# First batch's normalisation in two operations, its dilated values used where they land, one tail load a batch, and a new table of biases

## The chip, the cores and the metric

The kernel runs on one core of one Trainium2 chip. The metric is the device time of one execution in microseconds, median of the runs. Five engines work side by side, each through its own queue of instructions in order: TensorE (PE; its weight loads are shown apart as PEld), VectorE (DVE), ScalarE (ACT), GpSimd (POOL) and SyncE (SP). Loads are issued by POOL or SP and carried out by 16 DMA engines.

## The reference, cut to what matters

Attention over 8 batches, 8 heads, 576 positions and 64 columns a head, followed by a gated two-layer network over the 4608 tokens. Heads 0 to 3 see the 32 last positions ("plain"), heads 4 to 7 every fourth of the last 128 ("dilated").

```python
mask_plain = (rel >= 0) & (rel < 32)
mask_dil = (rel >= 0) & (rel < 128) & (rel % 4 == 0)
...
scores = np.where(masks, q @ k.T / 8, -1e9)
attn = np.exp(scores - max); attn = attn / (attn.sum() + 1e-9)
x = attn @ v                               # to (4608, 512)
h = x @ w_in                               # 512 x 2048
out = (h / (1 + np.exp(-beta * h))) @ w_out    # 2048 x 512
```

## The kernel before, in words

All products are in bf16. The network works on nine tiles of 512 tokens. For each, `slot_h` (L892) makes 16 blocks of 128 of the 2048 hidden columns: four products with w_in (L901) into a bank of PSUM, a tanh on ACT (L910), a gate on DVE (L915). `block` (L924, `block_cols` L930) makes four blocks of 128 tokens of the output: 16 products with w_out (L936) in four parts, an evacuation (L951 or L953) and a store from SP (L956). For the first four blocks of the first tile, `slot_h` splits its products in three: rows 2 and 3 of xT (the dilated heads) first, then rows 0 and 1 for the first 288 columns, then for the rest, so that it can start before all of batch 0's attention is done.

`attention` (L551) computes one batch into xT, which is the network's transposed input. The steps bear names: K and Q are transposes of keys and queries on PE (L483 dilated, L493 plain) and their copies out of PSUM (L257); S are scores (L697 dilated, L761 plain, T at L666 for the tail, the last 16 positions of each of the four dilated streams) with an exponential on ACT (L633) and, from batch 1 on, a mask on DVE or POOL (L637). Batch 0 gets its mask as a product with an identity instead (L687, L747, L750). V are the products of the weights with the values (L802 dilated, L818 plain), U those of the tail (L787). The values have a column of ones behind their 64 columns, so the 65th column of the product is the sum of the weights. `normed` (L644) then makes, on DVE and as one operation, a reciprocal of that column (L652) and a product with it (L653). In the first two batches X and Y transpose the result on PE (L855, L870, L840) and copy it into xT (L257); later ones go by DMA.

The values come in three ways. `direct_vp` (L430) loads the plain ones and copies a halo of 32 rows. `direct_vd` (L446) loads the dilated ones into vd16, 64 columns wide without ones, and `spread` (L619) copies them into vd, whose rows are 80 wide and have the ones; for the tail it issues two small loads into vt, one for each of two residues (L449). All these loads are issued by POOL (L408). Batches 0 to 2 load keys and queries straight into st; in batch 0 the first keys come by SP. The w_in matrix comes in three loads (L967), w_out in two halves (L972).

The order of all this is not written out. Each operation is registered in a list with the engines that may do it and their costs, its dependences and a due time (vt). `Plan.run` (L73) plays the list through on a model: among the operations that could start on an engine within about 50 ns of the first, the one with the smallest due time is taken, and where an operation may run on two engines, that one is open which ends at most 100 ns behind the other. `NUDGE` (L48) adds a bias in ns to the start at which an operation is compared; its key is the operation's place in the order of registration. A load counts eight earlier loads of its queue: it waits for the eighth before it to have landed. Where PE would be idle early on, the planner puts in fillers, products of zeros (L1057, L1059). The due times of batch 0's loads are those in L963 to L976: w_in -7.3, -7.29, -7.28, w_out -7.235 and -7.19. Those of batch 1's come from `loads` (L999): first keys -7.25, first queries -7.24, plain keys -7.23, plain queries -7.22, dilated values -7.2. Number 199 of the list is batch 1's load of the plain queries, with a bias of -900; number 32 is the small identity ident_f, with -2500.

Of the kernel before, what the change touches and what calls it, by code (L numbers as in the profile page):

```python
# [40 lines left out]
class Plan:  # L41
# [6 lines left out]
    NUDGE = {6: 2500, 32: -2500, 44: 150, 45: -400, 58: -150, 72: 60, 76: -400, 88: -400, 96: 60,  # L48
        98: 150, 104: -2500, 105: 900, 107: 900, 161: 150, 167: 900, 172: 60, 173: 400, 199: -900,
        208: 150, 214: -400, 216: 2500, 221: 900, 223: 150, 234: -400, 238: -150, 239: 150,  # L50
        241: 150, 248: -60, 250: -2500, 257: -400, 259: -400, 264: 60, 275: 900, 277: 400,
        278: -2500, 279: 400, 292: -150, 311: 900, 318: -400, 323: 150, 326: -900, 329: 400,
        333: -400, 337: 60, 342: -900, 347: -400, 363: 2500, 364: -900, 365: -150, 367: -2500,
        372: 400, 379: 60, 380: -400, 383: -150, 390: 400, 392: -2500, 394: -400, 408: -150,
        415: -900, 425: -150, 494: -900, 500: -150, 519: 60, 526: 900, 528: -60, 529: 900,
        535: 900, 538: 2500, 553: 900, 589: -60, 597: -2500, 633: 2500, 661: -900, 663: 400,
        669: 2500, 671: 2500, 680: 400, 681: -400, 684: 150, 685: -150, 807: 400, 916: -60,
        943: 150, 948: 150, 1083: 2500}
# [140 lines left out]
def kernel(  # L199
# [215 lines left out]
    def direct_qk(b, z, h0, deps, vt):  # L415
        rows, n, dst = ((2 * GD, RD, std) if h0 else (P, RP, stp))
        src = bass.AP(tensor=(k, q)[z].tensor, offset=(k, q)[z][b, h0].offset,
                      ap=[[n * D, rows], [2 * S * D, 2], [1, n * D]])
        return load("POOL", (dst[z], src), deps, vt, 576, .41 if b or not (z and h0) else .29, lat=1100 if b else 1450)
# [26 lines left out]
    def direct_vd(b, deps, vt, tdeps=()):  # L446
        src = v[b, 4:8].rearrange("h (t T) d -> t h (T d)", T=C)[0:P]
        out = [load("POOL", (vd16_of[b].rearrange("p h T d -> p h (T d)"), src), deps, vt, 512, .39, lat=1450 if b < DIRECT else 4000, late=0 if b <= DIRECT else 4000)]
        for c in range(2):  # L449
            src = bass.AP(tensor=v.tensor, offset=v[b, 4].offset + ((P - WIN) * C + c) * D,  # L450
                          ap=[[2 * D, 2 * KTL], [S * D, 4], [1, D]])
# [51 lines left out]
    def war(*keys):  # L503
        return [o for key in keys for o in last.get(key, ())]
# [588 lines left out]
```

## Time and profile before

| | |
|---|---|
| median of 3 runs | 299.92 us (299.8 to 299.94) |
| the profiled execution | 299.95 us |
| its span | 298.3 us, granted clock 0.999 |
| TensorE busy | 293.0 us |
| VectorE, ScalarE, GpSimd busy | 186.1, 169.8, 90.4 us |
| products with w_in (L901), with w_out (L936) | 134.8, 136.6 us |
| DMA | 42.00 MB, mean 141 GB/s |

Times of rows are in microseconds from the start of the span; "x" is a count of instructions. A row of the timeline gives start, length, engine, line, operation and what it writes and reads; in brackets the idle time before it and what ended that. The chain that ended last is the sequence of work followed back from the end, each step to what released it. Lengths of products are records that overlap, so a group of four with 512 columns is listed as 1.04 us in the timeline and takes 0.86 us in the chain.

The loads of POOL land one behind the other; by their completion times in the trace (us): first queries 7.44, plain keys 8.95, plain queries 10.34, dilated values 11.74, plain values 12.67 and 13.64, w_in's first part 16.50, batch 1's plain queries 17.99, w_in's second and third part 20.50 and 25.43, batch 1's dilated keys 26.84, batch 0's two tail loads 27.18 and 27.56, batch 1's dilated queries 28.94, w_out's first half 34.77, batch 1's plain keys 36.01 and dilated values 37.33, w_out's second half 42.44.

### The profile page before, as it was taken

The page shows a single profiled execution, that of the slowest core. Times are in us where ns is not written, and L with a number is a line of the kernel's source. Part 1 is how long each engine was busy: PE and PEld are TensorE (multiplying, and loading weights), DVE is VectorE, ACT ScalarE, POOL GpSimd, SP SyncE. Part 2 cuts the span into 40 slices and gives each one's busy share as a digit, 9 for nine tenths or more (in the row PEclk, how much of TensorE's full clock was granted, in tenths as well). Part 3 has the DMA queues.
Part 4 walks back from the last instruction along what each step waited for, and adds up shares of the span by engine and source line. Part 5 has one row for each costly group of instructions (what it writes and reads, how often), then busy time and mean ns, then how long its engine had stood idle before and what let it go on. Part 6 is the DMA issues. An engine that isn't in the chain of part 4 may idle for free.

```text
span 298.3 us, 6224 instructions
## 1 busy us (share of the span) xinstructions
PE 293.0 (98%) x2424; PEld 149.8 (50%) x2424; DVE 186.1 (62%) x422; ACT 169.8 (57%) x308; POOL 90.4 (30%) x126
## 2 busy tenths in 40 slices
PE   8999999999999999999999999999999999999995
PEld 6765456545554445444544454445444444444454
DVE  4879668888767658774589358936891075433300
ACT  3768876867456738642487348634862376445311
POOL 8987354654283026600551065000100000000000
PEclk9999999999999999999999999999999999999999
DMA  7999999999979995999999989995115200010122
GB/s 150 187 208 202 206 196 210 154 163 184 185 124 226 151 199 124 171 136 240 184 188 155 200 174 196 162 186 147 38 31 124 73 0 36 35 37 37 63 76 73
DMA packets 111249, 42.00 MB, mean 141 GB/s; under 512 B 87620, under 2 KB 104596, under 8 KB 111220
## 3 DMA queue, kind: packets, MB, share of 16 engines
q0 software_dynamic: 60336, 18.58, 59.6%
q1 hardware_dynamic: 50740, 22.95, 36.4%
q8 instruction: 19, 0.31, 0.4%
q10 hardware_dynamic: 144, 0.07, 0.1%
q14 instruction: 10, 0.08, 0.1%
HBM read 37.76 MB, written 18.87 MB: 190 GB/s over the span
## 4 chain that ended last, share of the span: by engine, by line
PE 86%; DMA 8%; POOL 2%; DVE 1%; issue 1%; ACT 0%; POOLq 0%
PE bank L936 42%; PE bank L901 36%; DMA w_out_bf<-in_moe_w_out_dram 6%; DMA w_in_bf<-in_moe_w_in_dram 2%; PE bank L818 2%; PE bank L697 1%; PE bank L802 1%; PE bank L725 1%; POOL vp L408 1%; PE bank L787 1%; PE bank L666 0%; PE bank L761 0%; POOL st L408 0%; DVE g L915 0%; PE bank L493 0%
## 5 line engine op out<-in xcount | busy, mean ns | idle before, releaser
L936 PE MATMUL bank<-w_out_bf,g 128*128 128x512 bf16 (+2 forms) x608 | 136.6, 368 | 0.4 <-DMA w_out_bf<-in_moe_w_out_dram 0.4
L901 PE MATMUL bank<-xT,w_in_bf 128*128 128x512 bf16 (+2 forms) x584 | 134.8, 376 | 0.1
L915 DVE SCALAR_TENSOR_TENSOR g<-tnh,bank 128x512 bf16<-128x512 bf16 x144 | 96.5, 683 | 51.5 <-ACT tnh L910 50.3
L910 ACT ACTIVATE tnh<-bank,beta_half 128x512 bf16<-128x512 f32 x144 | 98.4, 690 | 53.2 <-PE bank L901 47.4
L901 PEld LDWEIGHTS <-w_in_bf 128*128 128x128 bf16 x584 | 55.1, 98 | 60.6 <-issue 0.2
L936 PEld LDWEIGHTS <-g 128*128 128x128 bf16 x608 | 55.2, 98 | 57.8 <-DMA w_out_bf<-in_moe_w_out_dram 0.5
L951 ACT ACTIVATE osb<-bank 128x512 f32<-128x512 f32 (+1 forms) x30 | 17.6, 592 | 34.1 <-PE bank L936 29.5
L633 ACT ACTIVATE ptd<-bank 128x512 bf16<-128x512 f32 x32 | 17.0, 600 | 21.4 <-PE bank L697 21.4
L633 ACT ACTIVATE pt<-bank 128x384 bf16<-128x384 f32 (+1 forms) x54 | 21.1, 463 | 6.5 <-PE bank L725 4.1
L637 DVE TENSOR_TENSOR pt<-pt,mask_n 128x384 bf16<-128x384 bf16 (+1 forms) x39 | 14.5, 378 | 12.1 <-ACT pt L633 11.6
L653 DVE TENSOR_TENSOR xsp<-bank,rcp 96x384 bf16<-96x384 f32 x32 | 17.7, 554 | 1.1
L637 DVE TENSOR_TENSOR ptd<-ptd,mask_d 128x512 bf16<-128x512 bf16 x25 | 10.9, 448 | 11.3 <-ACT ptd L633 10.4
L953 DVE TENSOR_SCALAR osb<-bank 128x512 f32<-128x512 f32 (+2 forms) x8 | 4.9, 607 | 20.5 <-PE bank L936 20.5
L652 DVE RECIPROCAL rcp<-bank 128x4 f32<-128x4 f32 (+2 forms) x72 | 12.8, 177 | 3.5 <-PE bank L818 1.4
L408 POOL DMA_DIRECT2D vt<-in_v_dram x16 | 13.7, 864 | 4.0 <-DMA w_out_bf<-in_moe_w_out_dram 2.9
L637 POOL TENSOR_TENSOR pt<-pt,mask_n 128x288 bf16<-128x288 bf16 (+1 forms) x7 | 5.3, 764 | 31.2 <-ACT pt L633 31.2
L653 DVE TENSOR_TENSOR xdm<-bank,rcp 128x256 bf16<-128x256 f32 x32 | 13.6, 424 | 1.1
L408 POOL DMA_DIRECT2D s<-in_k_dram x10 | 12.9, 1286 | 0.6 <-issue 0.6
L1015 POOL COPY pace<-xT 1x2 bf16<-1x2 bf16 x4 | 0.7, 176 | 39.2 <-DMA xT<-x 39.2
L408 POOL DMA_DIRECT2D s<-in_q_dram x10 | 12.2, 1220 | 0.1
L818 PEld LDWEIGHTS <-pt 128*128 128x128 bf16 x192 | 8.9, 97 | 4.4
L408 POOL DMA_DIRECT2D vp<-in_v_dram x9 | 10.2, 1129 | 1.0 <-DVE g L915 0.8
(113 smaller groups left out, 186.8 us busy)
## 6 DMA issues: line engine op xcount, KB each, us to landing
out_dram<-osb SPq DMA_DIRECT2D x35, 256.0 KB, 3.8
s<-in_q_dram POOLq DMA_DIRECT2D x10, 288.0 KB, 10.2
s<-in_k_dram POOLq DMA_DIRECT2D x10, 288.0 KB, 9.0
w_out_bf<-in_moe_w_out_dram POOLq DMA_DIRECT2D x2, 1024.0 KB, 17.4
vp<-in_v_dram POOLq DMA_DIRECT2D x7, 288.0 KB, 13.5
st<-in_q_dram POOLq DMA_DIRECT2D x6, 288.0 KB, 10.0
x<-xsp SPq DMA_DIRECT2D x12, 144.0 KB
st<-in_k_dram POOLq DMA_DIRECT2D x5, 288.0 KB, 13.2
```

Source lines behind the costliest of these rows:

```text
L408: {"POOL": nc.gpsimd, "SP": nc.sync}[queue].dma_start(out=out, in_=in_)
L633: nc.scalar.activation(out=w(), in_=sc(), func=ACT.Exp, scale=SCALE)
L637: E[e].tensor_tensor(out=w(), in0=w(), in1=m(), op=ALU.mult)
L652: nc.vector.reciprocal(out=r, in_=p[..., D])
L653: nc.vector.tensor_tensor(out=dst, in0=p[..., 0:D], in1=r.unsqueeze(len(p.shape) - 1).to_broadcast(list(p.shape[:-1]) + [D]), op=ALU.mult)
L818: nc.tensor.matmul(pv[:, a, h2, :], lhsT=lhs, rhs=vp[kv][:, (2 * x + h2) * NI + 3 * j + a, 0:D + 1], start=True, stop=True)
L901: nc.tensor.matmul(bank(g)[:, a:z], lhsT=w_in_bf[:, kt, fb * P:(fb + 1) * P], rhs=xT[:, kt, xo + a:xo + z], start=(i == 0 and kt == kts[0] ...
L910: nc.scalar.activation(out=th[:, 0:n], in_=bank(g)[:, 0:n], func=ACT.Tanh, scale=beta_half[:, fb:fb + 1])
L915: nc.vector.scalar_tensor_tensor(out=g_t[t % 2][:, fb, c0:c0 + n], in0=th[:, 0:n], scalar=1.0, in1=bank(g)[:, 0:n], op0=ALU.add, op1=ALU.mult)
L936: nc.tensor.matmul(bank(g)[:, lo:hi], lhsT=g_t[t % 2][:, fb, tb * P:(tb + 1) * P], rhs=w_out_bf[:, fb, lo:hi], start=(fb == 0), stop=(fb = ...
L951: nc.scalar.mul(out=ob[:, lo:hi], in_=bank(g)[:, lo:hi], mul=0.5)
L953: nc.vector.tensor_single_scalar(out=ob[:, lo:hi], in_=bank(g)[:, lo:hi], scalar=0.5, op=ALU.mult)
```

## The change

In batch 0 alone, the spread is left out: the dilated products read vd16 where the load put it, 64 columns wide, and a second product of one column, with the ones of vd, makes the sum. In batch 0 alone, `normed` registers the reciprocal and the product as two operations, and the product may also run on ACT, one instruction for each block of 64 columns. In all batches the two tail loads become one. Two rates by which the planner reckons loads of later batches are changed, and the table of biases is replaced as a whole, since the places in the list shift: by -1 behind the merged load of batch 0, by -2 behind its spread, and by up to +7 behind its nine split norms. In the new table neither ident_f nor batch 1's plain queries (now number 206) has an entry; batch 1's tail load (now 208) has 150.

```diff
-    NUDGE = {6: 2500, 32: -2500, 44: 150, 45: -400, 58: -150, 72: 60, 76: -400, 88: -400, 96: 60,
-        98: 150, 104: -2500, 105: 900, 107: 900, 161: 150, 167: 900, 172: 60, 173: 400, 199: -900,
...
+    NUDGE = {54: -900, 57: 60, 58: -150, 63: -60, 67: -150, 68: -150, 69: -60, 75: 900, 77: 400, 91: 60,
+        93: -2500, 95: -900, 97: -60, 121: 60, 125: 60, 139: -2500, 140: 150, 143: 60, 146: 60,
+        152: 150, 156: -400, 167: -60, 175: 900, 188: -60, 208: 150, 214: 400, 219: 400, 221: 150,
...
-        return load("POOL", (dst[z], src), deps, vt, 576, .41 if b or not (z and h0) else .29, lat=1100 if b else 1450)
+        return load("POOL", (dst[z], src), deps, vt, 576, .36 if b > 1 else .41 if b or not (z and h0) else .29, lat=1100 if b else 1450)
...
-        for c in range(2):
-            src = bass.AP(tensor=v.tensor, offset=v[b, 4].offset + ((P - WIN) * C + c) * D,
-                          ap=[[2 * D, 2 * KTL], [S * D, 4], [1, D]])
-            out.append(load("POOL", (vt_[b % 2][:, c, :, 0:D], src), list(tdeps), vt + (1.255 if b == 0 else .02 if b < DIRECT else 0) + .001 + .001 * c, 96, .3, lat=1100 if b < DIRECT else 4000, late=0 if b <= DIRECT else 4000))
+        src = bass.AP(tensor=v.tensor, offset=v[b, 4].offset + (P - WIN) * C * D,
+                      ap=[[2 * D, 2 * KTL], [D, 2], [S * D, 4], [1, D]])
+        out.append(load("POOL", (vt_[b % 2][:, :, :, 0:D], src), list(tdeps),
+                        vt + (1.255 if b == 0 else .02 if b < DIRECT else 0) + .001, 192, .3,
+                        lat=1100 if b < DIRECT else 4000, late=0 if b <= DIRECT else 4000))
...
-        o = plan.op([("POOL", 1100), ("DVE", 620), ("ACT", 1030)], spread,
-                    [ld["vd"][0], (fill3, fill4)[kv]] + war(("vd", kv)), vt, sbuf=True)
-        used("vd16" if b < DIRECT else ("st", kv), o)
-        wrote(("vd", kv))
-        vdeps["D"] = [o]
+        if b:
+            o = plan.op([("POOL", 1100), ("DVE", 620), ("ACT", 1030)], spread,
+                        [ld["vd"][0], (fill3, fill4)[kv]] + war(("vd", kv)), vt, sbuf=True)
+            used("vd16" if b < DIRECT else ("st", kv), o)
+            wrote(("vd", kv))
+            vdeps["D"] = [o]
+        else:
+            vdeps["D"] = [ld["vd"][0], fill3]
...
+            if b == 0:
+
+                def inverse(e):
+                    p = pv()
+                    nc.vector.reciprocal(out=flat if len(p.shape) == 3 else flat.rearrange("p (m h) -> p m h", h=2), in_=p[..., D])
+                inv = plan.op([("DVE", 150)], inverse, [vop], vt - .003, group=g)
+
+                def scaled(e):
+                    p, to = pv(), dst
+                    r = flat if len(p.shape) == 3 else flat.rearrange("p (m h) -> p m h", h=2)
+                    if e == "DVE":
+                        nc.vector.tensor_tensor(out=to, in0=p[..., 0:D],
+                                                in1=r.unsqueeze(len(p.shape) - 1).to_broadcast(list(p.shape[:-1]) + [D]),
+                                                op=ALU.mult)
+                        return
+                    for i in range(blocks):
+                        at = (i,) if len(p.shape) == 3 else divmod(i, 2)
+                        at = (slice(None),) + tuple(at)
+                        nc.scalar.activation(out=to[at], in_=p[at][:, 0:D], func=ACT.Copy, scale=flat[:, i:i + 1])
+                vdone[key] = plan.op([("DVE", 160 + 1.042 * blocks * D), ("ACT", 235 * blocks)], scaled,
+                                     [inv] + war(war_key), vt - .003, group=g)
+                return
...
-                            nc.tensor.matmul(pv[:, r, a], lhsT=ptd[:, x - 2, j, 2 * r + a],
-                                             rhs=vd[kv][:, 2 * (x - 2) + a, 2 * r + j, 0:D + 1],
+                            lhs, at = ptd[:, x - 2, j, 2 * r + a], (slice(0, P), 2 * (x - 2) + a, 2 * r + j)
+                            if b:
+                                nc.tensor.matmul(pv[:, r, a], lhsT=lhs, rhs=vd[kv][at][:, 0:D + 1], start=True, stop=True)
+                                continue
+                            nc.tensor.matmul(pv[:, r, a, 0:D], lhsT=lhs, rhs=vd16_of[b][at], start=True, stop=True)
+                            nc.tensor.matmul(pv[:, r, a, D:D + 1], lhsT=lhs, rhs=vd[kv][at][:, D:D + 1],
                                              start=True, stop=True)
-                vop = plan.op([("PE", 4 * mm(D + 1))], values, [sdone[x, j]] + vdeps["D"], vt, acquire=g)
+                vop = plan.op([("PE", 4 * mm(D + 1) + (0 if b else 100))], values, [sdone[x, j]] + vdeps["D"], vt, acquire=g)
                 used(("vd", kv), vop)
+                if b == 0:
+                    used("vd16", vop)
```

## The prediction

> **What bounds the kernel now.** I read the page first (busy shares), then the chain that ended last, in order of time, then the waits of TensorE, then the windows and the timeline of the first 60 us. The page's span and first row say which engine it is:
>
> ```profile
> span 298.3 us, 6224 instructions
> ...
> PE 293.0 (98%) x2424; PEld 149.8 (50%) x2424; DVE 186.1 (62%) x422; ACT 169.8 (57%) x308; POOL 90.4 (30%) x126
> ```
>
> TensorE is busy for all but 298.3 - 293.0 = 5.3 us. So a VectorE operation that the change saves in the middle of the run is worth nothing; only two things count: work on TensorE, and the places where TensorE idles or runs fillers. The chain in order of time, to the first w_out product:
>
> ```profile
> 9.58 6.91 DMA w_in_bf<-in_moe_w_in_dram
> 16.50 0.28 issue
> 16.78 17.99 DMA w_out_bf<-in_moe_w_out_dram
> 34.81 1.04 PE bank L936 x4
> ```
>
> After 34.81 the chain is nearly all TensorE. Before it the chain is a transfer: the first half of w_out lands at 34.8, and TensorE stands still for it. The waits of TensorE have it as the only one after the start of the dense part (us in all, times, longest):
>
> ```profile
> PE bank L936 <- DMA w_out_bf<-in_moe_w_out_dram: 0.4, 1, 0.4
> ```
>
> The windows of the prologue (busy us of each engine in 1 us, then clock, DMA share, GB/s) show who is short while batch 0's attention is computed:
>
> ```profile
> 14.00:15.00 1.00, 1.00 (x20) 0.64 (x16) 0.94 (x4) 0.55 (x3) 1.00 (x3) 1.00 1.19 205
> 15.00:16.00 1.00, 1.00 (x20) 0.82 (x16) 0.93 (x5) 0.88 (x3) 1.00 (x3) 1.00 1.22 198
> 16.00:17.00 1.00, 0.95 (x17) 0.65 (x14) 0.97 (x3) 1.00 (x5) 0.56 (x2) 1.00 1.21 205
> 17.00:18.00 1.00, 0.79 (x15) 0.56 (x11) 0.96 (x5) 0.28 (x1) 0.69 (x1) 1.00 1.23 205
> ```
>
> VectorE is at 0.93 to 0.97, ScalarE at 0.28 to 1.00, and TensorE's own busy time is partly filler. The timeline names the pieces (start, us):
>
> ```profile
> 12.03 0.43 DVE L257 COPY vd<-vd 128x1024 bf16<-128x1024 bf16 x1
> ...
> 15.52 0.82 PE L1059 MATMUL bank<-zero 128*128 128x256 bf16 x6
> ...
> 17.22 0.38 PE L1059 MATMUL bank<-zero 128*128 128x256 bf16 x2
> ...
> 18.03 0.48 PE L493 MATMUL bank<-ident_b,st 64*64 64x64 bf16 x36 [0.25 <-DMA st<-in_q_dram]
> ...
> 18.44 1.04 PE L901 MATMUL bank<-xT,w_in_bf 128*128 128x512 bf16 x4
> ```
>
> From 18.03 TensorE has useful work without a break, but for the 0.39 us before 34.81. So the prologue is bounded by VectorE and the order on TensorE, the stretch to 42 us by the transfers, and the rest by TensorE alone. What the change can win is (18.03 minus the new start of the unbroken work) plus 0.39.
>
> **The parts of the change.** The sum is made against the profiled execution, 299.95 us: span 298.3 and 1.65 around it. The median of the runs shown, 299.92, is the same within 0.03.
>
> *The spread of batch 0 goes* (the 0.43 us row at 12.03). It lay on VectorE between the last query copy (to 12.01) and the halo copy at 12.69, which waited 0.23 us for a load that landed at 12.67. The dilated values had landed at 11.74 by the completion times of the loads, so the first dilated products may start at about 11.9 instead of 12.57, and the first reciprocal at about 12.2 instead of 13.04. VectorE then runs without a gap to 19.15 in the trace of before, so its chain becomes 0.43 + 0.23 = 0.66 us shorter. Bounds: 0, if the norms are held up by the halo copies all the same, and 0.84 (13.04 - 12.2).
>
> *In its place, 16 products of one column* (the four dilated groups, four each, at new places beside the 64-column ones), each with a weight load of its own. No row shows a one-column product. The nearest is L802's own: in the dense part the chain has 8 of 65 columns in 0.24 us, 30 ns each with its weight load, so 16 cost at most 16 x 30 = 0.48 us; at least nothing, as they stand where TensorE runs fillers (L1059 at 12.10, 12.82, 15.52 and 17.22, 12 in all). Each group is done up to 4 x 30 = 0.12 us later, which VectorE, still busy with the group before, covers; without that cover the first group alone would cost 0.12. I take 0 for the end of the prologue. On this the Trainium skill speaks against the change: the page "TensorE: Matmul & The Clock Gate", section "Back-to-back issue gap", has about 81 ns per pair of a weight load and a 128-column product in a sustained stream, and a floor of about 25 ns for any small one. By the 81 the 16 would be an estimate of 1.3 us, by the 25 of 0.4 us; the row above, at 30 ns, stands by the floor.
>
> *Reciprocal and product in two operations, the product on VectorE or ScalarE.* On VectorE the same instructions remain (0.17 + 0.42 us for four blocks, 0.18 + 0.55 for six). What is new is that ScalarE may do the product: one instruction per block. No row shows that one; the nearest is ScalarE's copy of 128x64 from a bank, x2 in 0.45 us, so 0.23 us each: 0.9 us for four blocks and 1.4 for six, against 0.42 and 0.55. The planner gives it to ScalarE only if it ends there within 100 ns of VectorE by its own costs (235 ns a block), so rarely. Worth: between -0.4 (one product on ScalarE in the way of the exponentials) and +1.0 (two products off VectorE). I take 0.
>
> *One tail load a batch instead of two.* Same runs of 64 elements, same bytes; the two loads of batch 0 landed 0.34 and 0.38 us behind their forerunners, one of twice the size is 0.7 by these. It saves an issue on GpSimd, median 709 ns, in each batch. GpSimd's queue is also where a load waits until the eighth before it has landed: the tail load at 35.05 stood 2.9 us behind the landing of w_out. With one load fewer each later one looks one place further back, so w_out's issue no longer waits 0.44 us for w_in. But the queue has a backlog all the while (loads land one upon the other from 7.4 to 42.4 us), so an earlier issue moves no landing: 0, from 0 to 0.1.
>
> *New biases.* They decide the order and are the largest part. I counted the operations in their order of registration (the numbers shift by -1 behind the merged load, -2 behind the spread, +7 behind the nine split norms) to see whose biases go. Two matter. (a) Number 199, batch 1's first plain query load, had -900 and jumped ahead of w_in's second and third parts; its successor, 206, has none. By due times alone the order becomes w_in (three), key, tail, query, w_out, key, query. That load took 1.49 us of the stream (17.99 after 16.50), so w_in's parts land at 19.0 and 23.9 instead of 20.50 and 25.43, and w_out's first half at 34.77 - 1.49 = 33.3. Its 0.48 us of transposes (L493 at 18.03) leave the prologue, but TensorE needs them later all the same. (b) Number 32, the small identity, lost its -2500, so the first load goes out about 0.8 us earlier; but by the packets in the trace SP's key load fills the DMA engines until 4.5 us, and the sum of both stays: 0, from -0.4 to +0.3. In the other stages biases trade one place for another; the cost of an unlucky swap is 0.11 us (L936 x4 takes 0.97 instead of 0.86 us in the chain where the operation before it had another form). Some five more or fewer give ±0.5, and I take 0.
>
> **The sum.** The earliest start of w_in's products is the landing of its first part, 16.5, plus 0.1. In the trace of before it was 18.03 with the transposes: (2,3) columns of xT were written by 17.78, late because the transposes of the last dilated pair (L855 at 16.53) stood behind a plain pair in TensorE's order, while its norm had ended at 15.64. With VectorE 0.66 us ahead I expect the start at 17.4: 0.6 us won, between 0 and 1.4. The wait of 0.39 us goes: TensorE would want w_out at 34.42 - 0.6 - 0.48 = 33.3, and it lands at 33.3; without (a) it would land at 34.8 and eat everything won. w_in's third part is wanted at 25.6 - 0.6 - 0.48 = 24.5 and lands at 23.9. Together 0.6 + 0.39 = 1.0 us: 299.95 - 1.0 = 298.95, so 298.9 on the scale of the medians. The likeliest case's own range is 298.1 to 299.3 (0.6 to 1.8 us).
>
> **Rivals.** *The transfers hide it* (27%): w_in or w_out keep their landing times since the query load stays ahead, and TensorE waits where it now arrives earlier. For it: the stream is full from 2 to 42 us, at about 200 GB/s in every window. Against: the lost bias. Gain 0 to 0.6 us, so 299.3 to 300.0; about 299.7.
>
> *Batch 1 starves* (12%, slower): the query load is not merely behind w_out's first half but behind its second, which lands at 42.44. Before, the plain scores of batch 1 began when the key load landed at 36.01, and the first w_in product of token tile 1 came at 52.09. TensorE then had three groups of w_out left as a reserve, and they came later:
>
> ```profile
> 52.09 0.97 PE bank L901 x4
> ...
> 59.30 0.86 PE bank L936 x4
> ...
> 61.15 0.86 PE bank L936 x4
> ...
> 63.00 0.86 PE bank L936 x4
> ```
>
> That is 2.6 us of cover. A landing before 36.01 + 2.6 = 38.6 costs nothing; at 42.44 it costs 42.44 - 38.6 = 3.8 us, less the 1.0 won: about 302.7. It decides by which of the two comes first in GpSimd's queue; the due times (-7.22 against -7.19) speak against it.
>
> *The order on TensorE or ScalarE is worse* (5%): products on ScalarE push exponentials back, 0.3 to 0.8 us: 300.2 to 300.7. *More than I count* (3%): under 298.1, if steady stages gain too. The forecast itself has 53%.
>
> The range leaves out starvation, the bad order and the surplus, 20% together: 298.1 to 300.1. This kernel's measurement tells about 0.2% (0.6 us) from no change: below 299.3 is faster, 56%; within, 29%; slower, 15%.
>
> **What would show it.** No DVE copy into vd near 12; the first batch's L802 doubled in number; the first L901 products at 17.0 to 17.8; the first plain query load of batch 1 issued behind w_out's first half; w_out landing near 33.3 and no wait of L936 on it; the dense part from there as long as before (295.2 - 34.8 = 260.4 us, plus the 0.5 of transposes, less what is done ahead). Wrong, if the first L901 stands at 18 or later, if L901 or L936 waits for a load, or if TensorE idles between 50 and 60 us.

## The result, and the profile after

The changed kernel takes 302.18 us (median of 4 runs, 301.54 to 302.63) against 299.93 for the kernel before: a ratio of 1.0071, 95% interval 1.0056 to 1.0085. It is slower by 2.2 us; the prediction was 298.9. The profiled execution took 301.86 us with a span of 300.1. One kernel below, the third of the "three guesses", was granted a lower clock in five of its six runs (0.984 to 0.994), so only its profiled one is read. In this profile the w_out product is L969 (L936 before), the w_in product L934 (L901), the plain scores L788 (L761), the dilated values L831, or L833 and L834 in batch 0 (L802), the filler L1092 (L1059).

The span and the engines' row of the changed kernel:

```profile
span 300.1 us, 6238 instructions
...
PE 293.9 (98%) x2440; PEld 150.8 (50%) x2440; DVE 185.8 (62%) x420; ACT 171.2 (57%) x312; POOL 83.0 (28%) x115
```

VectorE's and ScalarE's sums have hardly moved. TensorE's is 0.9 us longer, with 16 products more (those of one column); the fillers of 256 columns are 39 in both kernels. The timeline of TensorE around the start of the dense part and around 41 us (start, us, engine, line, operation):

```profile
16.75 0.38 PE L1092 MATMUL bank<-zero 128*128 128x256 bf16 x2
17.02 1.02 PE L934 MATMUL bank<-xT,w_in_bf 128*128 128x512 bf16 x4
...
33.24 1.03 PE L969 MATMUL bank<-w_out_bf,g 128*128 128x512 bf16 x4
...
38.80 0.48 PE L495 MATMUL bank<-ident_b,st 64*64 64x64 bf16 x36
...
40.54 0.48 PE L495 MATMUL bank<-ident_b,st 64*64 64x64 bf16 x36
...
41.08 0.60 PE L1092 MATMUL bank<-zero 128*128 128x256 bf16 x4
...
42.07 0.50 PE L1092 MATMUL bank<-zero 128*128 128x256 bf16 x3
```

The same stretch in the kernel before has no filler:

```profile
36.91 0.48 PE L493 MATMUL bank<-ident_b,st 64*64 64x64 bf16 x36
...
38.41 0.43 PE L761 MATMUL bank<-qT,kT 64*128 64x96 bf16 x12
...
42.74 1.89 PE L936 MATMUL bank<-w_out_bf,g 128*128 128x512 bf16 x8
```

The first w_in product now starts at 17.02, not after the transposes at 18.03, and the first w_out product at 33.24, not 34.81. But seven fillers stand at 41.08 to 42.42: TensorE is out of work there, where the kernel before had none. The waits of TensorE (us in all, times, longest):

```profile
PE bank L934 <- DMA xT<-x: 0.8, 1, 0.8
PE bank L1017 <- POOL ident_f masks.py:199: 0.5, 1, 0.5
PE bank L934 <- DVE g L948: 0.3, 1, 0.3
PE bank L851 <- DVE vp L258: 0.2, 1, 0.2
```

The wait on w_out is gone, as predicted. A wait on xT is new; it lies at 112.5, in the middle of the run (0.98 us by the spacing of the products). The windows show three stretches, first before, then changed (busy us of PE, PEld, DVE, ACT, POOL with counts, then clock, DMA share, GB/s):

```profile
36.00:48.00 12.00, 12.00 (x194) 6.50 (x194) 7.92 (x23) 8.79 (x22) 6.77 (x9) 1.00 1.63 190
70.00:92.00 22.00, 22.00 (x212) 11.44 (x207) 16.74 (x45) 13.07 (x27) 12.47 (x15) 1.00 1.06 173
110.00:125.00 15.00, 15.00 (x129) 7.54 (x128) 11.94 (x27) 10.34 (x19) 10.03 (x11) 1.00 1.00 166
```

```profile
36.00:48.00 12.00, 11.93 (x172) 6.55 (x170) 8.31 (x25) 8.10 (x21) 4.19 (x6) 1.00 1.77 185
70.00:92.00 22.00, 21.86 (x217) 11.41 (x214) 16.17 (x45) 11.44 (x25) 12.14 (x17) 1.00 1.22 172
110.00:125.00 15.00, 14.21 (x105) 6.92 (x103) 11.16 (x27) 9.67 (x18) 7.49 (x8) 1.00 1.07 146
```

Busy time alone hides fillers and stalls inside a group, so I made an account: the time that passed since TensorE's first product, at 1.13 us, less what the products issued so far need. Fillers count as lost. A product is taken to need its columns divided by 2.4 per ns, as the dense products of 512 columns follow one another every 216 ns in both traces; those of 64 rows start in pairs about 4 ns apart and are taken at half. TensorE's loss by stretch is then, before and after: to 36 us 11.66 and 11.00 (0.66 won), 36 to 48 us 1.00 and 1.92 (0.92 lost), 70 to 92 us 1.05 and 1.81 (0.76 lost), 110 to 125 us 0.62 and 1.33 (0.71 lost), elsewhere about 0.2 in all. All together it is 1.9 us, the difference of the two profiled executions (301.86 - 299.95). So the prologue brought what was forecast for it, and three later places cost 2.4 us. The first of them takes back the prologue's gain; at 60 us the changed kernel is 0.37 us behind, and most of the loss is made after that.

**What happened at 41 us.** The loads of the changed kernel land at 18.76 and 23.81 (w_in's second and third part), 32.35 (w_out's first half), 33.75 (batch 1's plain keys), 35.18 (its plain queries, 17.99 before), 41.61 (w_out's second half, 42.44 before). The query load has moved from ahead of w_out's first half to between the halves. The first half serves six groups of four products, since three open output blocks can take no more without the second half. Before, these six began at 34.81 and the seventh at 42.74; now they begin at 33.24 and the last of them at 39.46, but the second half lands only 0.83 us earlier. The stretch between the halves has to be filled with batch 1's attention, and that was late: its query transposes stand at 38.80 and its key transposes at 40.54, 3.6 and 6.8 us after their landings; before, the keys were transposed at 36.91, 0.9 us after their landing, and the plain scores began at 38.41 instead of 41.84.

### The profile page after: what moved, and what is told of

Read it like the earlier page. It is cut to its first block, busy times and chain, and to the rows that moved or that the text cites. A ratio compares the mean times of both kernels' runs of the same rounds, so it can differ in the third digit from the quotient of the medians.

```text
span 300.1 us, 6238 instructions
## 1 busy us (share of the span) xinstructions
PE 293.9 (98%) x2440; PEld 150.8 (50%) x2440; DVE 185.8 (62%) x420; ACT 171.2 (57%) x312; POOL 83.0 (28%) x115
## 3 DMA queue, kind: packets, MB, share of 16 engines
HBM read 37.76 MB, written 18.87 MB: 189 GB/s over the span
## 4 chain that ended last, share of the span: by engine, by line
PE 85%; DVE 4%; DMA 3%; SPq 2%; POOL 2%; issue 1%; ACT 1%; POOLq 0%; DVEq 0%; ACTq 0%
PE bank L969 39%; PE bank L934 35%; DMA xT<-x 3%; PE bank L851 2%; DVE g L948 2%; SPq L476 1%; PE bank L724 1%; PE bank L831 1%; SPq L549 1%; PE bank L752 1%; ACT tnh L943 1%; PE bank L495 1%; PE bank L814 1%; PE bank L788 1%; PE bank L1092 0%
## 5 line engine op out<-in xcount | busy, mean ns | idle before, releaser
L969 PE MATMUL bank<-w_out_bf,g 128*128 128x512 bf16 (+2 forms) x608 | 136.5, 368 | 0.0
L934 PE MATMUL bank<-xT,w_in_bf 128*128 128x512 bf16 (+1 forms) x584 | 134.9, 376 | 1.2 <-DMA xT<-x 0.8
L934 PEld LDWEIGHTS <-w_in_bf 128*128 128x128 bf16 x584 | 55.1, 98 | 61.8 <-DMA xT<-x 1.0
L969 PEld LDWEIGHTS <-g 128*128 128x128 bf16 x608 | 55.2, 98 | 57.4
L984 ACT ACTIVATE osb<-bank 128x512 f32<-128x512 f32 (+2 forms) x33 | 19.4, 588 | 42.5 <-PE bank L969 38.2
L658 DVE TENSOR_TENSOR xsp<-bank,rcp 96x384 bf16<-96x384 f32 x28 | 15.5, 554 | 1.2 <-DVE rcp L657 0.3
L657 DVE RECIPROCAL rcp<-bank 128x4 f32<-128x4 f32 (+2 forms) x63 | 11.3, 180 | 7.5 <-PE bank L831 4.0
L986 DVE TENSOR_SCALAR osb<-bank 128x512 f32<-128x512 f32 (+1 forms) x5 | 3.0, 610 | 20.7 <-PE bank L969 20.7
L409 POOL DMA_DIRECT2D s<-in_q_dram x10 | 13.1, 1309 | 0.0
L658 DVE TENSOR_TENSOR xdm<-bank,rcp 128x256 bf16<-128x256 f32 x28 | 11.9, 424 | 1.0
L409 POOL DMA_DIRECT2D vp<-in_v_dram x9 | 10.9, 1216 | 0.5 <-DMA st<-in_k_dram 0.5
L851 PE MATMUL bank<-vp,pt 128*128 128x65 bf16 x192 | 10.1, 193 | 0.3 <-DVE vp L258 0.2
L831 PEld LDWEIGHTS <-ptd 128*128 128x128 bf16 x112 | 6.4, 98 | 5.1
```

What stands on the lines that cost most here:

```text
L409: {"POOL": nc.gpsimd, "SP": nc.sync}[queue].dma_start(out=out, in_=in_)
L657: nc.vector.reciprocal(out=r, in_=p[..., D])
L658: nc.vector.tensor_tensor(out=dst, in0=p[..., 0:D], in1=r.unsqueeze(len(p.shape) - 1).to_broadcast(list(p.shape[:-1]) + [D]), op=ALU.mult)
L831: nc.tensor.matmul(pv[:, r, a], lhsT=lhs, rhs=vd[kv][at][:, 0:D + 1], start=True, stop=True)
L851: nc.tensor.matmul(pv[:, a, h2, :], lhsT=lhs, rhs=vp[kv][:, (2 * x + h2) * NI + 3 * j + a, 0:D + 1], start=True, stop=True)
L934: nc.tensor.matmul(bank(g)[:, a:z], lhsT=w_in_bf[:, kt, fb * P:(fb + 1) * P], rhs=xT[:, kt, xo + a:xo + z], start=(i == 0 and kt == kts[0] ...
```

## The experiments

For most of these kernels the planner's choice is replaced by a written list of steps, each a letter for the engine (T TensorE, A ScalarE, D VectorE, P GpSimd, S SyncE) and the number of the operation; biases then play no part. So an order can be given to either code, and single operations moved. "Order of before" and "new order" are the lists which the planner had made for the two kernels. Line numbers in the rows of such kernels lie 42 to 45 higher. The cuts of lists show only the engines that matter, with "..." where steps are left out. The kernel before took 300.02 to 300.22 us (medians) beside them, and ratios are to it.

**The parts of the change without its order.** The code of the change, in the order of before: first all three parts, then the single tail load, then the direct use of the dilated values.

```diff
-        while n_left:
-            best = None
+        for step in ORDER.split():
```

> The three parts of the change in the code (no spread in batch 0 and the one-column products, reciprocal and product as two operations, one tail load a batch), but every engine's operations and the fillers in the order that the kernel before has. If the order of the new table is what costs, this is 299.4 to 300.0 us, ratio 0.998 to 1.000: the dilated products and norms of batch 0 start up to 0.6 us earlier, but the plain query load of batch 1 still stands in front of w_out and w_in's later parts, so little of it is kept. If the parts themselves cost (the 16 one-column products, or the one larger tail load that lands later), it is 301 us or more.

> The kernel before, in its own order, with the two tail loads of each batch as one and nothing else. By the loads' landings 299.8 to 300.2 us, ratio 0.999 to 1.001: the same runs of 64 elements, one issue of 0.7 us less on GpSimd. If fewer places in GpSimd's queue make loads wait less: up to 0.4 us faster. If one load of twice the size delays the second residue: slower by 0.3 us or more.

> The kernel before, in its own order, with batch 0's spread left out and its dilated values used where they land (the 16 one-column products included), and nothing else. If the prologue's end follows VectorE's chain: 0.3 to 0.6 us faster, 299.4 to 299.7. If the order on TensorE holds the later steps where they were: 299.8 to 300.2. If the one-column products cost: 300.3 or more.

Measured: all three 300.02 us, ratio 0.9996 (0.9983 to 1.0009); the tail load 300.19, 1.0000 (0.9992 to 1.0009); the direct values 299.95, 0.9997 (0.9988 to 1.0005). The parts neither cost nor bring anything that can be measured (the intervals allow 0.5 us less to 0.3 us more; the split norms ran only together with the other parts). What the change costs is its order. Nor does the earlier start of the dense part come from the parts: with the spread left out in the order of before, the first w_in product stands at 19.25 us in the profile of the direct values and at 18.87 in that of all three (18.44 before). In both VectorE then waits for the halo's load, 0.85 and 0.84 us instead of 0.23, and TensorE has batch 1's query transposes ahead of w_in; in the first it waits 0.72 us for their load.

**The late query load by itself.** Before's code and order; batch 1's plain query load goes behind w_out's first half and the plain keys, its transposes with it, and two query loads of batch 2 follow it.

```diff
-P26 P10 P199 P27 P28 ... P29 P198 P11
+P26 P10 P27 P28 ... P29 P198 P199 P11
-T106 T94 T215 T116 ... T114 T184 T213
+T106 T94 T116 ... T114 T184 T215 T213
```

> The code and the order of the kernel before, with one thing moved as the changed kernel has it: batch 1's plain query load is issued behind w_out's first half and the plain keys, its transposes and copies stand in front of those of the keys on TensorE, and the two loads of batch 2's queries that overwrite the same tiles follow. If the late query load is the root of the loss: the prologue and the wait for w_out give 0.5 to 1.0 us, but batch 1's plain scores and token tile 1's first product come 1 to 2 us later than 38.4 and 52.0, and the whole is 300.3 to 301.5 us. If the query load is innocent and the loss lies in the later order alone: 299.0 to 299.5 us.

Measured: 303.36 us, ratio 1.0117 (1.0098 to 1.0136). Its first two waits of TensorE:

```profile
PE bank L536 <- DMA st<-in_q_dram: 1.7, 1, 1.7
PE bank L944 <- DMA xT<-x: 1.5, 1, 1.5
```

The first wait is not for the moved load itself but for a load of batch 2's queries that was moved along with it:

```profile
36.73 0.83 PE L536 MATMUL bank<-ident_b,st 64*64 64x64 bf16 x72
...
48.47 0.48 PE L536 MATMUL bank<-ident_b,st 64*64 64x64 bf16 x36 [1.66 <-DMA st<-in_q_dram]
```

The moved load landed at 36.20, and its transposes ran with those of the keys at 36.73. The load of batch 2, issued at 37.56 instead of 28.29, landed at 48.42, and TensorE waited 1.7 us for it; later it waited 1.5 us for batch 3's results. With its followers, moving this load back is a loss of 3.3 us in the order of before, where I had counted a gain. The stretch between w_out's halves is as long here as in the changed kernel (first product at 34.65, second half landed at 42.88: 8.2 us, against 8.4), and there is no filler and no wait in it. So it can be filled although the query load is late; the transposes stand at 36.73 here, at 38.80 and 40.54 in the changed kernel.

**Mending the order at 41 us.** First: the fillers go, and the first product on w_out's second half (T181) comes ahead of plain scores. Second: the query load goes back behind w_in's third part, its transposes early, the plain scores up.

```diff
-T268 T280 T242 T247 T283 T181 T252
+T268 T280 T181 T242 T247 T283 T252
```

> The changed kernel, but without the seven fillers between 41.1 and 42.5 us, and with the first product group that needs w_out's second half in front of the first plain scores of batch 1 instead of behind the second. If TensorE is idle there because the order waits for a landing later than the real one (41.6 us): 0.8 to 1.3 us faster than the changed kernel, 300.9 to 301.4, if the later waits stay as they are. If it is truly short of work, or if the gain only lengthens the later wait on xT: no faster than 301.8.

```diff
-P26 P27 P203 ... P205 P6 P206 P11
+P26 P27 P206 P203 ... P205 P6 P11
-T167 T155 T211 ... T191 T121 T221
+T167 T155 T221 T211 ... T191 T121
```

> The changed kernel with batch 1's plain query load issued behind w_in's third part and in front of the dilated keys, its transposes on TensorE at about 26 us instead of 38.8, the key's transposes at 37 instead of 40.5, and the plain scores of batch 1 moved up by as much; the fillers of 41 to 42.5 us are gone. If the late query load is the root of the loss: token tile 1's first tanh comes at 52.5 to 53.5 us instead of 55.2, w_out's first half lands at 33.8 and costs up to 0.6 us, and the whole is 299.5 to 300.8 us, 1.4 us or more below the changed kernel. If the loss lies in the order of the later batches alone: 301.7 or more.

Measured: 303.17 us, 1.0105 (1.009 to 1.012), and 302.71 us, 1.0086 (1.0071 to 1.0101). Both theories missed. The first waited 0.8 us for w_out's second half: the work put forward had not landed. It also met a wait that the changed kernel doesn't have, 1.4 us for a copy of batch 3's keys:

```profile
PE bank L735 <- POOL dkt L300: 1.4, 1, 1.4
...
PE bank L1011 <- DMA w_out_bf<-in_moe_w_out_dram: 0.8, 1, 0.8
```

The second had no fillers at 41 us, but its ninth tanh came at 28.25 instead of 26.55, and tile 1 began no earlier (first tanh 55.89, 55.22 in the changed kernel). By the account it loses 2.17 us from 36 to 48 us, more than the changed kernel (1.92) and twice as much as the kernel before (1.00).

**Is it that load's transfer?** The same load cut to 1 of 128 rows, in three orders.

```diff
+        if b == 1 and z and not h0:
+            src = bass.AP(..., ap=[[n * D, 1], [2 * S * D, 2], [1, n * D]])
+            return load("POOL", (dst[z][0:1], src), deps, vt, 576, .41, lat=1100)
```

> Control. Before's code and order, but batch 1's load of the plain queries brings 1 of its 128 rows, so that batch 1's plain heads are computed from batch 0's queries (left out: the rest of the load). Both theories: the stream of loads is some 1.5 us shorter from 18 us on and w_out's first half lands at 33.3 instead of 34.8, so that the wait of 0.39 us on it goes. 299.5 to 300.1, ratio 0.998 to 1.000.

> The same cut in the kernel query_early_new_order (changed kernel, query load behind w_in's third part, 302.7 us). Theory (the 1.5 us of this load's transfer is what the stretch to 42 us can't place; wherever it stands TensorE lacks a matrix or batch 1's scores): the 1.7 us that it lost at w_in go, w_out's second half lands at some 40.1 us, and what is left over before are the later stalls: 301.0 to 301.7. Rival (the places of the operations on TensorE cost it, not the transfer): 302.3 to 302.9.

> The same cut in the kernel reserve_first (303.2 us, which waited 0.8 us for w_out's second half and 1.4 us for a copy of GpSimd). Theory (transfer): the wait of 0.8 us goes, and part of what the late plain scores cost: 301.5 to 302.4. Rival (order): the wait moves to the plain scores, as their transposes stand where they stood: 302.9 to 303.3.

Measured: order of before 299.71 us, 0.9982 (0.9959 to 1.0004), as expected. New order with the load early 302.72 us, 1.0074 (1.0048 to 1.0101): the same as with the whole load, and the ninth tanh is at 28.25 again, so that delay comes from the order on TensorE, not from the transfer. With w_out's second half put forward 302.19 us, 1.0067 (1.0044 to 1.0091): the wait of 0.8 us on w_out is gone, and about 1.0 us of the time with it. So in reserve_first the landing of w_out's second half was one limit. But by the account both kernels still lose 2.16 and 2.00 us from 36 to 48 us, with the short load and without fillers; the last one waits 0.6 us for exponentials of the late plain scores. No run here won back the loss at 41 us.

That last kernel showed something else. The timeline of TensorE at 112 us, first with the load cut, then reserve_first:

```profile
112.02 0.62 PE L769 MATMUL bank<-dq,dk 64*128 64x128 bf16 x16
114.98 1.25 PE L979 MATMUL bank<-xT,w_in_bf 128*128 128x512 bf16 x5 [2.34 <-DMA xT<-x]
```

```profile
114.42 0.62 PE L766 MATMUL bank<-dq,dk 64*128 64x128 bf16 x16
115.13 1.04 PE L976 MATMUL bank<-xT,w_in_bf 128*128 128x512 bf16 x3
```

It came to the same scores 2.40 us earlier, and started on batch 3's results 0.15 us earlier. The rest went into the wait for xT. In this pair a gain before 112 us doesn't pass this point. (The changed kernel itself comes to these scores at 112.13; reserve_first was late by its wait of 1.4 us at 80.)

**Three guesses at the later stalls.** Batch 3's plain key cast ahead of its values; batch 3's loads let go by tile 0's last gate; batch 4's loads let go by a gate of tile 1 and put ahead of a mask. (From batch 3 on the keys and queries come by "casts", loads of GpSimd that leave them in memory as bf16; transposing loads of SyncE fetch them from there. The results go to memory too and come back into xT by transposing loads of SyncE. A small copy on GpSimd, "pace", waits for the results of the batch two before, for batch 3 for a gate of the network, and lets a batch's casts go.)

```diff
-P530 P532 P534 P528
+P530 P532 P528 P534
-S529 S447 S446
+S446 S529 S447
```

> The changed kernel, but GpSimd issues batch 3's plain key load in front of its values (as the kernel before does), and SyncE issues batch 2's second plain result store in front of the transpose that waits for that key load. If the chain key load, transpose on SyncE's queue, store, transposed result of batch 2, loads of batch 4, transposed result of batch 3 is what makes TensorE wait 0.8 us at 113: batch 2's last transposed result lands 3 us earlier than 87.7, the wait at 113 goes, and the time is 0.8 to 1.2 us less than the changed kernel, 301.0 to 301.4. If the transposes' own queue time sets it: 302.0 to 302.5, as before.

```diff
-    xT[0:1, 0, mid - 1:mid + 1] if b - 2 >= BY_DMA else g_t[b % 2][0:1, 0, 0:2]))
+    xT[0:1, 0, mid - 1:mid + 1] if b - 2 >= BY_DMA else g_t[0][0:1, NFB - 1, 0:2]))
```

> The changed kernel, in its own order, but the copy on GpSimd that holds back batch 3's loads reads the last gate of token tile 0 (about 33 us) instead of the first of tile 1 (56.8 us). If the 2 us by which tile 1 starts late are handed on through this copy to batch 3's loads, SyncE's queue, batch 2's transposed result and from there to the wait on xT at 113: batch 3's loads go out some 2 us earlier or more, that wait goes, and the time is 0.8 to 1.5 us below the changed kernel, 300.7 to 301.4. If not: 301.8 or more.

```diff
+    g_t[1][0:1, 11, 0:2] if b == 4 else xT[...] if b - 2 >= BY_DMA else ...
-P560 P662 P663 P665 P671 P673 P672 P669 P667
+P662 P663 P665 P671 P673 P672 P669 P667 D560
```

> The changed kernel with batch 4's loads let go by a gate of token tile 1 (about 81 us) instead of by xT of batch 2 (88.0 us), and put ahead of a mask on GpSimd, which goes to VectorE. Theory: the casts of batch 4 then end before SP transposes the results of batch 3 (from 100 us), these transposes land sooner, and the stall of 0.98 us at 112.5 us goes: 301.2 to 301.6. Rival: the transposes are late for another reason, and the stall stays or moves: 302.0 to 302.5.

Measured: 305.18 us, 1.0171 (1.0155 to 1.0188), and 302.45 us, 1.0078 (1.0065 to 1.009): both theories fell. In the first TensorE waits 1.6 us for batch 3's transposed plain keys at 86 us and 1.3 us for its results at 117. In the second batch 3's loads went out at 50.4 us instead of 56.9 and batch 4's still at 88.2. The third took 303.63 us in its profiled execution, above both ranges, and 307.5 to 312.9 in the others. There batch 4's casts were issued from 83.18 instead of 88.25, GpSimd's copy that waits for batch 3's results came at 112.28 instead of 113.64, and TensorE didn't wait for them, but batch 2's results, whose transposing loads were issued at 81.2 and 83.3, now stopped TensorE:

```profile
93.07 12.26 PE L976 MATMUL bank<-xT,w_in_bf 128*128 128x512 bf16 x56 [1.67 <-DMA xT<-x]
```

In the changed kernel the same two went out at 82.0 and 84.4 and had landed by 87.9. So the transposing loads of the one batch or of the other land late when casts are issued beside them (9.8 us after the last issue here, 3.5 there): each of these two choices of time cost one.

**The casts of batch 4 taken out.** The two plain casts of batch 4 reduced to one position, its plain heads fed from batch 3's. Nothing is moved.

```diff
+        if b == 4 and not h0:
+            args = tuple(x[0:1] for x in args)
+            scratch[b, z, h0] = scratch[3, z, h0]
```

> The changed kernel, in which batch 4's two plain casts bring one position instead of 576 and batch 4's plain heads take batch 3's keys and queries (left out: the rest of these two loads). Nothing else is moved. Theory (in the changed order TensorE is held at 112.5 us by the results of batch 3, whose transposing loads land late because they stand behind batch 4's casts in the DMA engines): xT lands before 112.5 us, the stall of 0.98 us goes and is not given back: 301.0 to 301.4. Rival (the transposes are late on their own, by SP's issue at 103.4 us and their own length): 302.0 to 302.5.

> Control: the same cut in before's code and order. There TensorE doesn't wait for batch 3's results, so both theories: 299.8 to 300.3, ratio 0.999 to 1.001.

> The kernel small_query_reserve_first (302.2 us, in which TensorE was 2.4 us earlier at 112 us than in reserve_first and then waited 2.3 us for batch 3's results) with batch 4's plain casts cut as well. Theory (two limits one behind the other: what is won before 112 us is lost again in the wait for batch 3's results): the 2.3 us go, 299.9 to 300.5. Rival: the wait stays, 301.8 to 302.4.

Measured: new order 301.54 us, 1.0050 (1.0029 to 1.0070); order of before 300.22, 1.0000 (0.9988 to 1.0013); both cuts in reserve_first's order 302.07, 1.0063 (1.0033 to 1.0093). The windows of the changed kernel, then of the one with the small casts:

```profile
104.00:108.00 4.00, 4.00 (x20) 1.83 (x19) 0.97 (x3) 0.08 (x1) 0.00 (x0) 1.00 1.72 157
108.00:112.00 4.00, 4.00 (x20) 1.70 (x18) 1.47 (x3) 1.59 (x3) 0.00 (x0) 1.00 1.77 158
```

```profile
104.00:108.00 4.00, 4.00 (x20) 1.80 (x19) 1.29 (x3) 0.00 (x0) 0.00 (x0) 1.00 1.24 184
108.00:112.00 4.00, 4.00 (x20) 1.84 (x19) 1.65 (x3) 1.67 (x3) 3.35 (x6) 1.00 1.30 166
```

```profile
113.64 0.31 POOL L1048 COPY pace<-xT 1x2 bf16<-1x2 bf16 x1 [10.41 <-DMA xT<-x]
```

```profile
108.33 0.18 POOL L1093 COPY pace<-xT 1x2 bf16<-1x2 bf16 x1 [4.62 <-DMA xT<-x]
```

The share of the DMA engines falls, xT has landed at 108.3 instead of 113.6 (by the copy on GpSimd that waits for it), and the stall at 112.5 is gone. Up to the 49th tanh this execution is 0.32 us behind the changed kernel's, from the 50th on 0.54 ahead: 0.86 us won in this place. The median is 0.6 us below that of the changed kernel, and the two intervals overlap a little: the landing and the stall are shown, the size in the time is about 0.6 to 0.9. The control moved nothing. In the kernel before, batch 4's casts go out from 83.55 us (88.25 in the changed kernel) and have landed by 109.1, and TensorE starts on batch 3's results at 110.91 without a wait. Why they go out 4.7 us later, behind batch 2's results, is not shown; the run meant for it, the first of the guesses above, was slower still. The third kernel does not settle its question: its twelve runs lie between 300.48 and 304.81, and its profiled one (303.10) met, ahead of the place in question, the wait of 1.57 us for batch 3's dilated keys that its sibling's profile does not have. It came to batch 3's results at 115 us, when they had been there since 110.5.

**The stall at 74 us.** One operation moved: GpSimd's copy into vd, behind three other copies.

```diff
-P425 P419 P539 P538 P536 P535 P551
+P425 P419 P538 P536 P535 P539 P551
```

> The changed kernel with one operation moved: GpSimd's copy into vd at 73.38 us goes behind its three small copies that follow it. Theory: that copy slowed VectorE's mask of the same time from 0.37 to about 1.03 us and with it the plain products at 74.4 and 74.9 us; without it the stalls of 0.46 us go: 301.7 (301.5 to 301.9). Rival: the masks are late on their own account (ScalarE's exponentials), or another of GpSimd's copies does the same: 302.1 to 302.3.

Measured: 302.15 us, 1.0080 (1.0048 to 1.0112). VectorE's two masks of that moment in the changed kernel, then in this one:

```profile
73.64 1.38 DVE L642 TENSOR_TENSOR pt<-pt,mask_n 128x288 bf16<-128x288 bf16 x2
```

```profile
73.69 0.53 DVE L684 TENSOR_TENSOR pt<-pt,mask_n 128x288 bf16<-128x288 bf16 x2
```

The mechanism was right: 1.38 us become 0.53, and the plain products at 74.4 take 0.53 instead of 1.00 us. Of the time only a part came: behind 74 us this execution gains 0.47 us on the changed kernel's by its tanh operations, and at 112 us, where TensorE waits 1.01 us for xT instead of 0.79, it gives back 0.22. What is left, 0.2 us of the profiled execution (301.65 for 301.86), is below what the medians can tell.

**The two halves of the order.** The new order for what starts before about 52 us and the order of before for the rest, and the reverse.

In short (the kernels hold the lists written out):

```diff
-ORDER = new
+ORDER = [x for x in new if x.start < 52] + [x for x in old if x not in first]
```

> The changed kernel, with its own order for all operations that it starts up to about 52 us and the order of before for the rest. Theory (two separate losses: TensorE short of work at 41 us, and two stalls at 74 and 113 us that belong to the later order): at 60 us the changed kernel was 14.67 - 14.30 = 0.37 us behind, and nothing is lost behind that, so 300.4 us (300.1 to 300.8). Rival (one loss that carries on: batch 1's late queries push every later load and transpose back, and these make the stalls at 74 and 113 us whatever the later order): 301.8 to 302.2.

> The mirror of the other splice: the order of before up to about 52 us, the changed kernel's for the rest. Theory (separate losses): the 0.76 us of 70 to 92 us and the 0.71 us of 110 to 125 us stay, so 300.0 + 1.5 = 301.5 (301.1 to 301.8). Rival (the first loss carries on): 300.0 to 300.3. If both splices are near 300, the two halves only cost together.

Measured: 301.95 us, 1.0063 (1.0042 to 1.0084), and 302.31 us, 1.0070 (1.0045 to 1.0095). The first lies in the range of its rival, the second above both of its ranges, so neither theory holds for the pair: each half costs about as much as both together. The first has no wait at 113 us, but others that neither parent has: 0.38 us at 68.86 for results on VectorE and 0.74 at 78.40 for batch 3's dilated keys, whose casts went out from 58.25 us (55.04 before). In the second the wait for a copy of batch 3's keys costs 0.9 us at 79.25. That each half is late for loads which the other order times otherwise is a reading of these waits; no run tests it.

## Why the prediction was wrong, point by point

Two terms of the sum failed: the 0.39 us booked for the new biases, and the 0 taken for the order of the other stages. The rest came out, one part of it for another reason.

- *The prologue.* The number was right: the unbroken work began at 17.02 (I had 17.4, and 17.0 to 17.8 as the sign), and by 36 us TensorE had lost 0.66 us less than before. The reason was not. I had it from the end of the spread, by VectorE's chain; but with the spread left out in the order of before the dense part began at 18.87 and 19.25: VectorE waited for the halo's load instead, and TensorE had batch 1's query transposes ahead of w_in. All profiled kernels with the order of before, changed in places or not, began it at 18.44 to 19.26, all with the new order at 17.02 to 18.11. The new order takes batch 1's query transposes out of the way and, with the spread gone, lets the first reciprocal (12.48) run ahead of the halo copy (13.24). VectorE did all nine products; ScalarE none.
- *Sixteen one-column products.* Right at 0: they follow the 64-column ones at 0.03 us each and stand among fillers, as the row of 65 columns had said; the 81 ns that the Trainium skill has for a pair with a 128-column product (page "TensorE: Matmul & The Clock Gate", section "Back-to-back issue gap") are not the price of these.
- *One tail load, ident_f.* Right at 0. The merged load landed 0.63 us after its forerunner, as estimated from 0.34 and 0.38. ident_f was later, and TensorE waited 0.5 us for it at 9.37; the first dilated products at 12.00 waited for their load all the same, which landed at 11.95. The first load went out 0.2 us earlier (1.39 for 1.58), not 0.8.
- *New biases, (a).* Here it failed. The landings were right (w_in at 18.76 and 23.81 for 19.0 and 23.9, w_out even at 32.35 for 33.3) and so was the end of the 0.39 us wait. I booked that as a gain and asked of the moved load only whether it landed before 38.6. But a load moved back in a full stream is not gone: it went between the halves of w_out, so the second half came only 0.83 us earlier than before, while the first half was taken up 1.57 us earlier, and the six groups that the first half allows ran out first. That stretch had to be filled with batch 1's attention, and its transposes stood 3.6 and 6.8 us behind the landings, which the sum had no term for. Instead of 0.39 won, 36 to 48 us cost 0.92 more.
- *Batch 1 starves.* The rival's condition did not occur: the load landed at 35.18, well before my point of decision, and TensorE ran short nevertheless. The "reserve of three groups" needs w_out's second half, which wasn't there; and I had let the plain scores of before begin at the landing of their keys (36.01), where they began at 38.41. By the traces what counted was where the transposes stand on TensorE, in an order that the planner makes by its own model of the landings. That the rival's 302.7 lies near the 302.18 is luck: it had 3.8 us lost here, and 0.92 were.
- *"In the other stages biases trade one place for another", ±0.5, taken as 0.* It measured 0.76 + 0.71 = 1.5 us lost, of stalls that I had not priced at all. At 74 us a mask of VectorE stood beside a copy of GpSimd; at 112 us batch 3's results landed late. In the runs above a swap did not cost the 0.11 us of a change of form, but a wait of 0.4 to 1.7 us wherever a load or a copy came late.
- *Transfers behind 42 us.* I had called the rest bounded by TensorE alone. At 112 us in the changed order TensorE waits for the results' transposing loads.

What stays open: how the 2.2 us divide. The stall at 112 us is worth some 0.6 to 0.9 us by the run without it, the one at 74 us 0.47 in its place, of which about half was lost again at 112; the loss at 41 us is read from the traces, as no run removed it. No order that I tried on the changed code beats both kernels; the order of before on it ties (0.9996).

## What to carry to other kernels

In a stream of loads that is full, moving one load back moves others too: follow it to the loads that it now delays or splits, and ask what the engine does between two landings, and where in its order the work stands that could fill them. Where an engine is 98% busy, price a change of order at the waits that it may open, not at the changes of form; separate code from order by replaying the old order on the new code. And look for the next place that everything waits for, since a gain ahead of it may reach the end only in part.

## What the runs showed of the hardware

Two masks of VectorE (128x288, bf16) took 1.38 us beside a copy of GpSimd (128x1024, 1.12 us) and 0.53 us without it; the slow one of the two took 1.03 us and ended 0.16 us behind the copy. Transposing loads landed later with casts in the DMA engines: those of batch 2 landed 3.5 us after their last issue with the casts issued behind them (84.4 to 87.9), those of batch 3 about 10 us after it with the casts beside them (103.4 to 113.4, in windows with 157 and 158 GB/s), and by 108.3 (last issue 103.6) when two of the casts were all but taken out.
